# A decay table spread over 128 partitions: eight DMAs out of SBUF rows instead of one out of DRAM

## The chip, the core and the metric

The program runs on one core of a Trainium2 chip. The metric is the device time of one execution in microseconds (us). Engines are named as in the profile: PE is TensorE, DVE is VectorE, ACT is ScalarE, POOL is GpSimd, SP is SyncE; the last issues DMAs here and computes nothing.

## The reference, cut to what matters

Three parts run one after another. First comes retention attention with a decay `lam[h]` for each of 8 heads; then a mixture of 8 experts over 1536 tokens; then a two-layer network. Only the first touches the change:

```
Dmask = where(rel >= 0, lam[h] ** rel, 0)        # rel = i - j, inside a block
intra = (q_b @ k_b^T) * Dmask ; intra @ v_b
inter = (q_b * lam[h] ** (i + 1)) @ kv_state
kv_state = lam[h] ** block * kv_state + (k_b * lam[h] ** (block - 1 - j))^T @ v_b
```

The kernel uses blocks of 128 positions, which gives the same output.

## The kernel before, in words

Attention works on 12 chunks, each a block of 128 positions of all 8 heads for one of the two batches. A chunk's input is one tile `qkv` of 128 partitions by 4 x 512 floats (q and k laid out with head dimension on the partitions, then k and v with positions on the partitions; 1 MB). Four such tiles exist, so the load of chunk c + 4 is issued once `outputs(c)` has freed a tile. `load_chunk` (L169) issues a chunk in two pieces of 512 KB; chunk 0 comes as two pieces of 256 KB (q and the first k) and, later, one of 512 KB (the second k and v). All DMAs of the kernel are issued by SP, in program order, on one queue.

The decays are tabulated at the start. `g` is a tile of 8 partitions, one per head, by 384 floats: 128 zeros, then 1, then the powers lam, lam^2, ... made by one scan on DVE (L190). From it come two tables over many partitions:

- `dtab` (L196), 128 partitions x 8 heads x 128 floats, 512 KB: partition j of head h holds the 128 floats of `g`'s row h that begin at column 1 + j. So each partition reads the same row, shifted by one float.
- `lq` (L203), 128 partitions x 4 x 128 floats, 256 KB: each head's powers, the same on 64 partitions.

Neither can be read by a single DMA across `g`'s partitions in this form, so `g` is stored to a DRAM tile `gscr` (L194), and `dtab` and `lq` are read back from there.

`dtab` is used by each chunk in two places: `decay` (L242, DVE) multiplies the scores in PSUM by it, and `prep` (L227, POOL) multiplies the second k by its last column. In a chunk PE runs `scores` (L236), `states` (L258, which needs `prep`'s k), and `outputs` (L272, L277, which needs `decay`'s product). While PE has no chunk it runs matmuls on zeros, 12 at the start (L182) and 10 after the first scores (L358).

The order of the work is written out by hand; each engine runs its instructions in program order, and the framework adds the semaphore waits. From chunk 1 on, the preparation of the expert layers (splitting tokens and weights into high and low parts, L132, L133; sums of weight blocks, L109 to L112) is put between the chunks. The expert layers start on PE at L579 once the last chunks are done.

The lines of the start, in the order in which SP issues them:

```
nc.sync.dma_start(out=lamt, ...)          # L166
load_chunk(0, ((0, 1), (1, 2)))           # L176
nc.sync.dma_start(out=gscr, in_=g)        # L194
load_chunk(0, ((2, 4),))                  # L195
nc.sync.dma_start(out=dtab, in_=...gscr)  # L198
load_chunk(1)                             # L202
nc.sync.dma_start(out=lq[...], ...gscr)   # L206, twice
load_chunk(2); load_chunk(3)              # L210
nc.sync.dma_start(out=wgt, ...)           # L212
```

Of the kernel before, what the change touches and what calls it, by code (L numbers as in the profile page):

```python
# [8 lines left out]
F32 = mybir.dt.float32  # L9
# [8 lines left out]
B, H, S, D = 2, 8, 768, 64  # L18
# [32 lines left out]
def kernel(  # L51
# [9 lines left out]
    nc = tc.nc  # L61
# [20 lines left out]
    gscr = dram.tile([H, 384], F32, name="gscr")  # L82
# [78 lines left out]
    ap = attq.enter_context(tc.tile_pool(name="att", bufs=1, side="right"))  # L161
# [7 lines left out]
    def load_chunk(c, parts=((0, 2), (2, 4))):  # L169
        if c not in qkvt:  # L170
            qkvt[c] = yq.tile([128, 4, 512], F32, tag="qkv", name=f"qkv{c}")
        src = qkv[c].rearrange("p (a n) -> p a n", a=4)
        for i, j in parts:
            nc.sync.dma_start(out=qkvt[c][:, i:j], in_=src[:, i:j])
# [6 lines left out]
    for i in range(12):  # L181
        nc.tensor.matmul(out=warm, lhsT=zero[:, 0:128], rhs=zero, start=True, stop=True)  # L182
    g = hp.tile([128, 512], F32, tag="hhi", name="g")[0:H, 0:384]
# [7 lines left out]
        out=g[:, 129:257], data0=lamt.to_broadcast([H, 128]), data1=one8, initial=1.0,  # L191
        op0=ALU.mult, op1=ALU.add,
    )
    nc.sync.dma_start(out=gscr, in_=g)  # L194
    load_chunk(0, ((2, 4),))  # L195
    dtab = ap.tile([128, H, 128], F32, name="dtab")  # L196
    gbase = gscr[:, 1:129]
    nc.sync.dma_start(  # L198
        out=dtab,
        in_=bass.AP(tensor=gbase.tensor, offset=gbase.offset, ap=[[1, 128], [384, H], [1, 128]]),  # L200
    )
    load_chunk(1)  # L202
    lq = ap.tile([128, NP, 128], F32, name="lq")  # L203
    for hh in range(2):
        src = gscr[:, 129:257].rearrange("(n two) m -> two n m", two=2)[hh]
        nc.sync.dma_start(  # L206
            out=lq[64 * hh:64 * hh + 64],
            in_=src.rearrange("(o n) m -> o n m", o=1).to_broadcast([64, NP, 128]),
# [537 lines left out]
```

## Time and profile before

| what | value |
|---|---|
| median of 3 runs | 1327.33 us (1326.79 to 1328.92) |
| the profiled execution's own time | 1328.56 us |
| its span, first to last instruction | 1326.8 us |
| PE busy | 1314.7 us (99% of the span) |
| DVE busy | 913.0 us (69%) |
| ACT, POOL busy | 527.6 us (40%), 274.6 us (21%) |
| DMA traffic | 85.00 MB, mean 64 GB/s |

The engines' shares are means over the whole span. The attention part with its loads takes about the first 60 us; after it PE is busy almost without a gap until the end. The span leaves out 1.8 us of the profiled execution's time that lie before the first and after the last instruction.

### The profile page before, as it was taken

The page shows a single profiled execution, that of the slowest core. Times are in us where ns is not written, and L with a number is a line of the kernel's source. Part 1 is how long each engine was busy: PE and PEld are TensorE (multiplying, and loading weights), DVE is VectorE, ACT ScalarE, POOL GpSimd, SP SyncE. Part 2 cuts the span into 40 slices and gives each one's busy share as a digit, 9 for nine tenths or more (in the row PEclk, how much of TensorE's full clock was granted, in tenths as well). Part 3 has the DMA queues.
Part 4 walks back from the last instruction along what each step waited for, and adds up shares of the span by engine and source line. Part 5 has one row for each costly group of instructions (what it writes and reads, how often), then busy time and mean ns, then how long its engine had stood idle before and what let it go on. Part 6 is the DMA issues. An engine that isn't in the chain of part 4 may idle for free.

```text
span 1326.8 us, 20925 instructions
## 1 busy us (share of the span) xinstructions
PE 1314.7 (99%) x8383; PEld 1163.6 (88%) x8383; DVE 913.0 (69%) x1698; ACT 527.6 (40%) x1029; POOL 274.6 (21%) x323
## 2 busy tenths in 40 slices
PE   8999999999999999999999999999999999999998
PEld 6789999999999999999999999999999888888887
DVE  4976666757667575767666675757654487788887
ACT  1443333223323232323322332323232578776764
POOL 4611011212123131212212221322210102020200
PEclk8999999999999999999999999999999999999999
DMA  9501111212312121212222132221210110010101
GB/s 299 171 33 33 33 61 34 71 56 68 97 46 93 57 68 57 80 56 68 72 64 68 57 99 69 68 68 57 68 36 33 32 33 32 32 32 32 32 33 64
DMA packets 37138, 85.00 MB, mean 64 GB/s; under 512 B 4136, under 2 KB 13872, under 8 KB 37040
## 3 DMA queue, kind: packets, MB, share of 16 engines
q1 hardware_dynamic: 37040, 83.67, 19.8%
q8 instruction: 65, 1.06, 0.3%
q14 instruction: 33, 0.27, 0.1%
HBM read 72.11 MB, written 11.55 MB: 63 GB/s over the span
## 4 chain that ended last, share of the span: by engine, by line
PE 96%; DVE 2%; DMA 1%; issue 0%; ACT 0%; POOL 0%; DVEq 0%; POOLq 0%
PE yp L480 16%; PE yp L477 16%; PE yp L478 16%; PE ha L579 7%; PE ha L582 7%; PE ha L581 7%; PE hb L581 5%; PE hb L579 5%; PE hb L582 5%; PE g L688 3%; PE g L686 3%; PE g L687 3%; PE sc L236 1%; DMA dtab<-gscr 0%; DVE at L242 0%
## 5 line engine op out<-in xcount | busy, mean ns | idle before, releaser
L508 ACT ACTIVATE hhia<-ha 128x512 fp32r<-128x512 f32 x96 | 57.5, 599 | 469.9 <-PE ha L582 464.3
L579 PE MATMUL ha<-xsh,w1h 128*128 128x256 f32 x576 | 162.5, 282 | 1.8 <-ACT s L600 1.3
L582 PE MATMUL ha<-xsh,w1l 128*128 128x256 f32 x576 | 161.3, 280 | 0.0
L581 PE MATMUL ha<-xsl,w1h 128*128 128x256 f32 x576 | 160.9, 279 | 0.0
L456 POOL TENSOR_TENSOR c<-c,d 128x256 f32<-128x256 f32 x64 | 47.8, 747 | 544.3 <-DVE d L455 544.3
L478 PE MATMUL yp<-w2l,hhia 128*128 128x512 f32 x384 | 149.4, 389 | 0.0
L480 PE MATMUL yp<-w2h,hloa 128*128 128x512 f32 x384 | 149.3, 389 | 0.0
L477 PE MATMUL yp<-w2h,hhia 128*128 128x512 f32 x384 | 149.3, 389 | 0.0
L480 PE MATMUL yp<-w2h,hlob 128*128 128x512 f32 x380 | 148.6, 391 | 0.0
L478 PE MATMUL yp<-w2l,hhib 128*128 128x512 f32 x380 | 147.9, 389 | 0.0
L477 PE MATMUL yp<-w2h,hhib 128*128 128x512 f32 x380 | 147.8, 389 | 0.0
L615 DVE TENSOR_TENSOR ha<-ha,s 128x256 f32<-128x256 f32 x96 | 41.4, 432 | 141.8 <-PE ha L582 141.8
L625 DVE TENSOR_TENSOR hb<-hb,s 128x512 f32<-128x512 f32 x96 | 67.0, 698 | 91.3 <-PE hb L582 91.3
L495 DVE SCALAR_TENSOR_TENSOR yacc<-yp,prob,yacc 128x512 f32<-128x512 f32 x168 | 118.8, 747 | 9.0 <-PE yp L480 9.0
L579 PEld LDWEIGHTS ha<-xsh,w1h 128*128 128x128 f32 x576 | 108.4, 188 | 9.6 <-ACT s L600 1.5
L581 PEld LDWEIGHTS ha<-xsl,w1h 128*128 128x128 f32 x576 | 108.5, 188 | 7.4
L582 PEld LDWEIGHTS ha<-xsh,w1l 128*128 128x128 f32 x576 | 109.1, 189 | 0.0
L579 PE MATMUL hb<-xph,w1h 128*128 128x256 f32 x384 | 106.6, 278 | 0.0
L581 PE MATMUL hb<-xpl,w1h 128*128 128x256 f32 x384 | 106.3, 277 | 0.0
L582 PE MATMUL hb<-xph,w1l 128*128 128x256 f32 x384 | 106.1, 276 | 0.0
L480 PEld LDWEIGHTS yp<-w2h,hloa 128*128 128x128 f32 x384 | 72.1, 188 | 15.0
L480 PEld LDWEIGHTS yp<-w2h,hlob 128*128 128x128 f32 x380 | 71.3, 188 | 14.9
(159 smaller groups left out, 3332.6 us busy)
## 6 DMA issues: line engine op xcount, KB each, us to landing
wraw<-in_w SPq DMA_DIRECT2D x64, 512.0 KB, 4.8
d<-in_wio SPq DMA_DIRECT2D x64, 256.0 KB, 2.9
qkv<-in_qkv SPq DMA_DIRECT2D x23, 512.0 KB, 6.9
wscr<-c SPq DMA_DIRECT2D x64, 128.0 KB, 1.8
wraw<-wscr SPq DMA_DIRECT2D x16, 512.0 KB, 4.3
out<-yacc SPq DMA_DIRECT2D x12, 256.0 KB, 2.1
qkv<-in_qkv SPq DMA_DIRECT2D x2, 256.0 KB, 3.3
dtab<-gscr SPq DMA_DIRECT2D x1, 512.0 KB, 6.5
```

Of the source, the lines that this page charges most:

```text
L456: nc.gpsimd.tensor_tensor(out=c1.bitcast(F32), in0=c1.bitcast(F32), in1=lo.bitcast(F32), op=ALU.mult)
L477: nc.tensor.matmul(out=yp, lhsT=a[:, ts], rhs=w2h[q][:, i], start=first, stop=False)
L478: nc.tensor.matmul(out=yp, lhsT=a[:, ts], rhs=w2l[q][:, i], start=False, stop=False)
L480: nc.tensor.matmul(out=yp, lhsT=c[:, ts], rhs=w2h[q][:, i], start=False, stop=last)
L495: nc.vector.scalar_tensor_tensor(out=y, in0=yp[t], scalar=prob[:, b * TPB + t, u // 2:u // 2 + 1], in1=y, op0=ALU.mult, op1=ALU.add)
L508: nc.scalar.activation(out=a, in_=ps, func=ACTF.Relu)
L579: nc.tensor.matmul(out=ps, lhsT=w1h[q][:, ws], rhs=xh[:, k], start=start and k == 0, stop=False, skip_group_check=True)
L581: nc.tensor.matmul(out=ps, lhsT=w1h[q][:, ws], rhs=xl[:, k], start=False, stop=False, skip_group_check=True)
L582: nc.tensor.matmul(out=ps, lhsT=w1l[q][:, ws], rhs=xh[:, k], start=False, stop=k == 1, skip_group_check=True)
L615: nc.vector.tensor_tensor(out=pa[:, hi], in0=pa[:, lo], in1=s5, op=ALU.add)
L625: nc.vector.tensor_tensor(out=pb, in0=pb, in1=s12, op=ALU.add)
L686: nc.tensor.matmul(out=ph, lhsT=w1h[q][:, ws], rhs=x2[b][0][:, k], start=k == 0, stop=False)
```

## The change

`dtab` is no longer read from `gscr`. Eight DMAs, one for each head, read `g`'s row h in SBUF (one partition) and write all 128 partitions of `dtab[:, h]`, 128 pieces of 512 bytes, 64 KB. The even heads are issued by SP, the odd ones by ACT. They are issued right after the scan that makes `g`, ahead of the store to `gscr` and of the second half of chunk 0; `gscr` stays, since `lq` is read from it as before.

```diff
+    dtab = ap.tile([128, H, 128], F32, name="dtab")
+    for h in range(H):
+        w = g[h:h + 1, 1:129]
+        (nc.sync, nc.scalar)[h % 2].dma_start(
+            out=dtab[:, h], in_=bass.AP(tensor=w.tensor, offset=w.offset, ap=[w.ap[0], [1, 128], [1, 128]]),
+        )
     nc.sync.dma_start(out=gscr, in_=g)
     load_chunk(0, ((2, 4),))
-    dtab = ap.tile([128, H, 128], F32, name="dtab")
-    gbase = gscr[:, 1:129]
-    nc.sync.dma_start(
-        out=dtab,
-        in_=bass.AP(tensor=gbase.tensor, offset=gbase.offset, ap=[[1, 128], [384, H], [1, 128]]),
-    )
     load_chunk(1)
```

## Rows read from the trace of the kernel before

**Rows 1.** The page's part 4: the chain that ended last, shares by engine.

```profile
PE 96%; DVE 2%; DMA 1%; issue 0%; ACT 0%; POOL 0%; DVEq 0%; POOLq 0%
```

**Rows 2.** Stretches: window and length, busy us (instructions), PE clock, DMA share, GB/s.

```profile
2.00:10.00 8.00, 6.80 (x37) 3.07 (x35) 0.55 (x2) 0.22 (x2) 0.00 (x0) 1.00 0.81 223
10.00:30.00 20.00, 17.06 (x261) 14.89 (x263) 10.13 (x18) 3.73 (x7) 13.91 (x14) 0.83 1.02 346
30.00:56.00 26.00, 24.94 (x434) 20.82 (x430) 25.78 (x39) 11.14 (x23) 19.07 (x16) 1.00 0.67 234
70.00:1320.00 1250.00, 1250.00 (x7510) 1112.50 (x7510) 862.78 (x1613) 504.49 (x983) 236.32 (x282) 1.00 0.17 55
```

**Rows 3.** The chain in order of time: start us, length us, what.

```profile
0.74 1.31 DMA lamt<-in_lam
...
2.59 2.62 DMA gscr<-g
...
5.22 6.46 DMA dtab<-gscr
...
11.83 1.07 POOL qkv L227
...
12.94 1.12 PE stp L258 x16
14.07 1.71 PE o L277 x16
15.77 2.01 PE sc L236 x16
17.78 0.69 PE stp L258 x16
18.47 1.09 PE sc L236 x16
19.56 1.02 PE o L277 x16
```

**Rows 4.** Timeline of the start: start, length, engine, line, tiles [idle before, releaser].

```profile
2.15 0.41 DVE L190 TENSOR_TENSOR_SCAN g<-lamt,one 8x128 f32<-8x128 f32 x1 [0.47 <-DMA lamt<-in_lam]
2.92 0.34 SPq L174 DMA_DIRECT2D qkv<-in_qkv  x1
5.65 1.18 SPq L174 DMA_DIRECT2D qkv<-in_qkv  x2
6.47 2.33 PE L358 MATMUL still<-zero 128*128 128x512 bf16 x10
15.37 1.06 POOL L227 TENSOR_TENSOR qkv<-qkv,dtab 128x512 f32<-128x512 f32 x1 [2.48 <-DMA qkv<-in_qkv]
15.82 0.60 ACT L291 ACTIVATE xr<-o 128x512 f32<-128x512 f32 x1 [13.59 <-PE o L277]
17.78 1.28 POOL L225 TENSOR_TENSOR qd<-qkv,lq 128x512 f32<-128x512 f32 x1 [0.35 <-DMA qkv<-in_qkv]
```

**Rows 5.** Stretches of 2 us; columns as in rows 2.

```profile
10.00:12.00 2.00, 0.00 (x0) 0.00 (x0) 0.22 (x1) 0.00 (x0) 0.17 (x1) 0.77 1.00 376
...
16.00:18.00 2.00, 2.00 (x22) 1.78 (x22) 0.18 (x1) 0.42 (x1) 1.26 (x3) 0.52 1.01 397
18.00:20.00 2.00, 2.00 (x42) 1.81 (x40) 1.51 (x3) 0.00 (x0) 1.99 (x2) 1.00 1.04 392
```

**Rows 6.** DMA between 8 and 9 us: packets by size, and the queue's share.

```profile
DMA packets 307, 0.16 MB, mean 157 GB/s; under 512 B 0, under 2 KB 307, under 8 KB 307
...
q1 hardware_dynamic: 307, 0.16, 75.9%
```

**Rows 7.** SP's waits in the first 40 us: us, times, longest.

```profile
SPq L212 <- DMA qkv<-in_qkv: 1.5, 1, 1.5
SPq L174 <- DMA dtab<-gscr: 1.2, 1, 1.2
```

**Rows 8.** POOL's waits in the first 60 us: us, times, longest.

```profile
POOL qd L225 <- DMA qkv<-in_qkv: 2.9, 3, 2.3
```

## The prediction

> **What bounds the kernel now.** I read the shares of the chain first, then stretches of the span, then the chain and the timeline of the start. The chain is PE's for 96% of the span [rows 1], and from 70 to 1320 us PE has no idle time at all [rows 2]. So nothing after the attention part can absorb or add much: whatever the change does to the moment at which the expert layers start is what it does to the total.
>
> The first 60 us have three regimes. Up to 12 us the chain is DMA: `lamt` lands, DVE makes `g`, `g` takes 2.62 us to DRAM, and `dtab` takes 6.46 us from its issue at 5.22 to its landing at 11.68; at 11.83 POOL starts the first `prep` [rows 3]. From 10 to 30 us the DMA engines are full (share 1.02, 346 GB/s) beside a PE that carries the chain [rows 2, 3]. From 30 to 56 us DVE is busy for 25.78 of 26 us and the DMA share falls to 0.67 [rows 2]. A shift of the first `prep` passes through all three: PE and DVE follow it with almost no slack, and the DMA engines have slack only before 10 us, where their share is 0.81 over 8 us, a gap of 0.19 x 8 = 1.5 us [rows 2].
>
> **What is removed.** The round trip: `dtab` no longer waits for the 2.62 us of `gscr`, and its own 6.46 us go [rows 3]. The store to `gscr` itself stays, and `lq` still waits for it.
>
> **What is added on the queues.** Eight issues, four each on SP and ACT. Neighbouring issues on SP cost 0.34 us, or 0.59 each in the pair that takes 1.18 [rows 4], so four cost 1.4 to 2.4 us. On ACT they are hidden: its first work on a chunk is at 15.82 after 13.59 us of idleness [rows 4]; without that cover they would delay the first `xr` copy by these 2 us. On SP they stand in front of `gscr` and of chunk 0's second half, issued at 2.92 before [rows 4], and nothing covers that: `prep` needs that half too. There is also a wait in turn: SP's second piece of chunk 3 waited 1.2 us for `dtab`, and `wgt` 1.5 us for a piece of `qkv` [rows 7]. In the list of issues each of these stands exactly eight behind what it waits for. If that count runs over both queues together, heads 6 and 7 wait for chunk 0's first pieces, and then `gscr`, chunk 0's second half and both pieces of chunk 1 wait for heads 0 to 3 to land, the `lq` reads for heads 4 and 5, chunk 2 for heads 6 and 7. So all loads hang on how fast the eight land.
>
> **What the eight reads cost.** No transfer of before goes from SBUF to SBUF, so I bound it. Each head moves 128 x 512 B = 65,536 B, all eight 524,288 B.
>
> Lower end: the rate of full loads, 392 GB/s [rows 5], gives 1.34 us. Next to it stands the rate of the same 512 B pieces as they come from DRAM: 307 in 1 us at 157 GB/s [rows 6], which gives 3.3 us.
>
> Upper end: the source is 8 of 128 partitions. In the full loads 128 partitions together take 392 GB/s [rows 5], so eight take a sixteenth, 24.5 GB/s, which is also one DMA engine's rate. No row shows eight partitions moving more. At that rate a head takes 2.67 us and all eight 21.4 us. Farther still, a single partition's share is 3.06 GB/s: if one head at a time went at that, the eight would take 171 us. And if small pieces held a shared source to what one engine does with them, 157 / 16 / 0.76 = 12.9 GB/s [rows 6], it would be 40.6 us.
>
> The destination and the pieces are as before; what is new is the source, 128 readers of one partition. So I go by the row on how many bytes a few partitions move, 24.5 GB/s for the eight, and take 21.4 us.
>
> The Trainium skill speaks against this change at the same place. Its page "SBUF — State Buffer", section "Door 1: The DMA port swizzle (why [64,N] ≈ [32,N])", says that a DMA's bandwidth follows from how many of SBUF's 16 ports its partitions reach, that partitions 0 to 3 lie behind one port and 4 to 7 behind another, and that four partitions were measured at 27.6 GB/s. By it heads 0 to 3 would take 262,144 B / 27.6 GB/s = 9.5 us and heads 4 to 7 as long again, 9.5 us if both halves ran at once and 19.0 us in the order of issue, an estimate. No run so far shows a read of so few partitions.
>
> **The sum.** `g` is ready at 2.56 us [rows 4]; the smallest DMA takes 1.31 us from issue to landing [rows 3], so data flow by 2.59 + 1.31 = 3.9 us. The eight are done at 3.9 + 21.4 = 25.3 us. Chunk 0's second half is behind them on the same queue: 524,288 B at 392 GB/s, 1.3 us, 26.6 us. `prep` followed the landing by 0.15 us [rows 3]: 26.8 us instead of 11.83, 15.0 us late. What is late next: chunk 1 is there at 26.6 + 2.7 = 29.3 us against 15.37 [rows 4], 13.9 late, which that shift covers; the `lq` reads (256 KB, about 0.8 us) and chunk 2 (2.7 us) end at about 32.8 us against 17.78 [rows 4], 15.0 late. All three agree, so the whole part moves by 15 us. PE idles longer, from the end of the zero matmuls at 8.80 [rows 4] to about 28 us, but its clock had already fallen in the short pause of before (granted 0.77 between 10 and 12, 0.52 between 16 and 18, 1.00 from 18 on [rows 5], that is to 1.2 GHz and back to 2.4), so the same slow stretch is paid again, not a new one.
>
> 1328.56 + 15.0 = 1343.6 us for an execution like the profiled one; that one lay 1.2 us above the median, so against the median I say **1342 us**, 1.1% slower.
>
> **Rivals.**
>
> *The rows are read at the rate of other transfers, and it is faster.* The place is `dtab`'s landing; the point that decides is 11.68 us, that is 524,288 B in 7.8 us, 67 GB/s, if chunk 0's second half comes in time too. For it: the 512 B pieces from DRAM, 1,536 B of one row shared by 128 readers there too, came at 157 GB/s [rows 6]. Against it: eight partitions. Then `dtab` lands at 3.9 + 1.3 to 3.3 = 5.2 to 7.2 us, chunk 0's second half, put back by the issues and the wait in turn, at perhaps 9, and `prep` starts 2.8 us earlier. PE's pause shrinks, and its slow stretch (1.12 + 1.71 + 2.01 us against 0.69 + 1.02 + 1.09 at full clock [rows 3]) can give back 2.0 more. But the loads from 10 to 30 us can come earlier only by what fills the gap before, 1.5 us, and POOL already waited up to 2.3 us for `qkv` [rows 8]. So 1.5 to 4.8 us, say 2.5: 1325 us.
>
> The Trainium skill has a rule on this side too: "DMA: Bandwidth & Descriptors", section "Why small descriptors are slow (HBM only)", says that SBUF to SBUF transfers do not suffer from small descriptors. By it the eight would come nearer to the 1.34 us of the full rate; the 512 B packets of rows 6 do run slow, and they come from DRAM, so the trace agrees as far as it goes.
>
> *Two rows are read at a time,* one from each queue, each at 24.5 GB/s: 10.7 us, `dtab` at 14.6, chunk 0's second half at 15.9, `prep` 4.2 us late: 1331.5 us. For it: the two queues are independent. Against it: the rows of the same moment are neighbours.
>
> *Nothing changes that can be measured:* a read of about 7 us ends where the old one did, or an earlier `dtab` is eaten by the later second half of chunk 0: 1326 to 1329 us.
>
> **The numbers.** Chances: 0.50 for the forecast or slower still, 0.13 for two rows at a time, 0.27 for the faster rival, 0.10 for no change. About 0.2%, 2.7 us, is what a measurement can tell from no change. The faster rival lies on that bound and is split, 0.16 beyond and 0.11 within; of the case without change 0.03 is slower. So faster 0.16, same 0.18, slower 0.66. The likeliest case's own range runs from 24.5 + a fifth, 29.4 GB/s (17.8 us, 3.6 less: 1338) to halfway between 24.5 and 12.9, 18.7 GB/s (28.0 us, 6.6 more: 1349). For 8 in 10 the range must take in the two-at-a-time case, no change and most of the faster one: 1324 to 1349. Some 0.1 lies below; 0.1 lies above, with the ends of 40.6 us and 171 us.
>
> **What would show it.** Right: `dtab`'s eight DMAs take several us each from issue to landing, in steps of some 2.7 us; POOL's first `prep` waits until past 20 us; the DMA rate between 4 and 25 us is a small part of 223 GB/s; afterwards chain and loads look as before, shifted. Wrong: `dtab` lands before 11 us and the wait in front of `prep` becomes one for `qkv`; or the rate of the eight is far from 24.5 GB/s; or part of the shift is taken back between 30 and 60 us, if DVE's stretch has more slack than 0.2 us.

## The result, and the profile after

The changed kernel takes 1341.54 us (median of 4 runs, 1340.27 to 1342.32) against 1327.37 us (4 runs, 1326.79 to 1328.92): a ratio of 1.0105, 95% interval 1.0092 to 1.0118, or 14.2 us. The profiled execution of after took 1341.58 us at a span of 1339.8 us, 13.0 us more than that of before.

The page's part 4 of the changed kernel. SP's issues have become a part of the chain, where before they were none [rows 1]:

```profile
PE 95%; DVE 2%; DMA 1%; SPq 1%; issue 0%; ACT 0%; DVEq 0%
```

Stretches of the changed kernel (columns as in rows 2). The first three cover the reads of the table; the last three answer to [rows 2], each 14 us later:

```profile
6.00:13.00 7.00, 2.91 (x22) 1.35 (x19) 0.00 (x0) 0.00 (x0) 0.00 (x0) 1.00 0.65 27
13.00:15.00 2.00, 0.00 (x0) 0.00 (x0) 0.00 (x0) 0.00 (x0) 0.00 (x0) 0.83 0.62 55
15.00:21.00 6.00, 0.00 (x0) 0.00 (x0) 0.00 (x0) 0.00 (x0) 0.00 (x0) 0.50 0.59 25
...
24.00:44.00 20.00, 16.57 (x250) 14.39 (x252) 9.00 (x17) 3.73 (x7) 13.41 (x13) 0.82 1.00 346
44.00:70.00 26.00, 24.69 (x440) 20.80 (x437) 25.90 (x39) 10.67 (x22) 18.93 (x17) 1.00 0.66 231
84.00:1334.00 1250.00, 1250.00 (x7505) 1112.70 (x7504) 862.07 (x1614) 503.90 (x981) 236.50 (x282) 1.00 0.17 55
```

The reader sees three things. From 6 to 21 us the DMA engines move 25 to 27 GB/s, and about twice that between 13 and 15, where the reads pass from the rows of heads 0 to 3 to those of heads 4 to 7. The share of busy time (0.59 to 0.65) does not show it: before, a share of 0.76 went with 157 GB/s [rows 6]. And the later stretches are nearly those of before, in rates and in busy times.

The timeline of the changed kernel's start (columns as in rows 4):

```profile
2.60 11.64 SPq L198 DMA_DIRECT2D dtab<-g  x4
2.61 8.73 ACTq L198 DMA_DIRECT2D dtab<-g  x4
...
14.29 4.34 SPq L201 DMA_DIRECT2D gscr<-g  x1
18.67 3.23 SPq L174 DMA_DIRECT2D qkv<-in_qkv  x3
...
23.32 1.29 DVE L243 TENSOR_TENSOR at<-sc,dtab 128x512 f32<-128x512 f32 x2 [20.60 <-DMA qkv<-in_qkv]
...
25.54 1.06 POOL L228 TENSOR_TENSOR qkv<-qkv,dtab 128x512 f32<-128x512 f32 x1 [24.09 <-DMA qkv<-in_qkv]
...
26.65 1.12 PE L259 MATMUL stp<-qkv 128*64 128x64 f32 x16 [17.74 <-POOL qkv L228]
...
30.03 1.06 POOL L228 TENSOR_TENSOR qkv<-qkv,dtab 128x512 f32<-128x512 f32 x1 [3.43 <-DMA qkv<-in_qkv]
...
32.43 1.27 POOL L226 TENSOR_TENSOR qd<-qkv,lq 128x512 f32<-128x512 f32 x1 [0.38 <-DMA qkv<-in_qkv]
```

The first `prep` starts at 25.54 us instead of 11.83 [rows 3], 13.7 us late; `prep` of chunk 1 at 30.03 instead of 15.37 and `qd` of chunk 2 at 32.43 instead of 17.78 [rows 4], 14.7 us late. Four issues hold SP for 11.6 us; the store to `gscr` and then chunk 0's second half come only after them. That half, not the table, is what the first `prep` waits for in the end: it lands 6.5 us after its issue, at 25.2 us. The last piece of the table to land is head 6, which SP issues at 10.46 us (issues between 10.6 and 11.2 us, with KB each and us to landing):

```profile
dtab<-g SPq DMA_DIRECT2D x1, 64.0 KB, 12.7
```

So the table is whole at 23.2 us. DVE's first product with it starts at 23.32; the profile puts that wait down to a load of `qkv`, but the scores that the product also needs had been ready since 6.6 us.

In the two profiled executions, a part of the shift is given back at the beginning of the expert layers. The chain of the changed kernel, and the same place in that of before (start, length, what):

```profile
78.70 0.39 PE ha L580
...
81.10 0.99 PE lgT L329 x32
```

```profile
64.16 0.39 PE ha L579
...
67.17 1.83 PE lgT L328 x32
```

At the first pair the shift is 14.54 us, at the second 13.93, and behind the second, whose work takes 0.84 us less, it is the 13.0 us of the span. The pause in front of the first pair is the same, 1.3 us of idle time in both (timelines of before and of after):

```profile
64.16 0.39 PE L579 MATMUL ha<-xsh,w1h 128*128 128x256 f32 x1 [1.32 <-ACT s L600]
```

```profile
78.70 0.39 PE L580 MATMUL ha<-xsh,w1h 128*128 128x256 f32 x1 [1.32 <-ACT s L601]
```

After it PE's clock fell to half (0.50, that is 1.2 GHz) in before and not in after (stretches of before, of after, and of the first experiment below, in which the eight read DRAM; columns as in rows 2):

```profile
66.00:68.00 2.00, 2.00 (x26) 1.55 (x29) 0.72 (x2) 1.31 (x3) 0.00 (x0) 0.50 0.00 0
```

```profile
80.00:82.00 2.00, 1.86 (x38) 1.54 (x38) 0.79 (x2) 1.86 (x4) 0.00 (x0) 1.00 0.04 8
```

```profile
66.00:68.00 2.00, 2.00 (x41) 1.65 (x40) 1.59 (x4) 1.66 (x5) 0.00 (x0) 1.00 0.04 8
```

Nothing shows that the change took that half clock away: the experiment's attention part is as early as that of before, and its clock does not fall there either. Of all the kernels profiled here, only before and the one with its rows in every fourth partition show it at this place. The profiled execution of before lay 1.2 us above its median, and by the medians the shift is 14.2 us, close to the 14.54 at the first pair.

### The profile page after: what moved, and what is told of

Same layout as the page of the kernel before. It is cut to its first block, busy times and chain, and to the rows that moved or that the text cites. A ratio compares the mean times of both kernels' runs of the same rounds, so it can differ in the third digit from the quotient of the medians.

```text
span 1339.8 us, 20940 instructions
## 1 busy us (share of the span) xinstructions
PE 1313.1 (98%) x8383; PEld 1163.2 (87%) x8383; DVE 912.5 (68%) x1698; ACT 527.9 (39%) x1029; POOL 274.7 (21%) x323
## 4 chain that ended last, share of the span: by engine, by line
PE 95%; DVE 2%; DMA 1%; SPq 1%; issue 0%; ACT 0%; DVEq 0%
PE yp L481 16%; PE yp L478 16%; PE yp L479 16%; PE ha L580 7%; PE ha L583 7%; PE ha L582 7%; PE hb L582 5%; PE hb L580 5%; PE hb L583 5%; PE g L689 3%; PE g L687 3%; PE g L688 3%; SPq L198 1%; DMA qkv<-in_qkv 1%; DMA gscr<-g 1%
```

## The experiments

Three theories stood against each other. Theory 1: the source is the limit, since few neighbour partitions together give some 25 GB/s. Theory 2: 128 readers of one row, each shifted by 4 bytes, are slow wherever the row lies. Theory 3: eight small DMAs from two queues are slow whatever they read, or SBUF is a slow source as such. Ratios are to the kernel before on the same chip.

| run | us | ratio, 95% interval |
|---|---|---|
| the eight read DRAM | 1326.88 | 0.9996 (0.9986 to 1.0005) |
| rows in partitions 0, 4, ... 28 | 1330.66 | 1.0028 (1.0018 to 1.0038) |
| no shift | 1341.76 | 1.0107 (1.0087 to 1.0127) |
| source of 128 partitions | 1326.69 | 0.9999 (0.9990 to 1.0009) |
| all eight from ACT | 1338.62 | 1.0081 (1.0064 to 1.0098) |
| rows in partitions 0 to 3 and 32 to 35 | 1345.72 | 1.0134 (1.0113 to 1.0156) |
| table by scan | 1324.06 | 0.9976 (0.9967 to 0.9985) |
| both tables by scan | 1322.53 | 0.9969 (0.9957 to 0.9980) |

**The eight read DRAM.**

```diff
-        w = g[h:h + 1, 1:129]
+        w = gscr[h:h + 1, 1:129]      # moved behind the store to gscr and chunk 0's second half
```

> The eight DMAs, their size and the two queues stay, but they read the heads' rows in gscr, in DRAM, after the store to it. Theory 1 (few partitions: the eight rows lie in 8 neighbour partitions, which together give about 25 GB/s): the source is gone, so the table lands within 2 us of before's 11.7 us and the time is that of before, 1325 to 1330 us. Theory 2 (128 readers of one row, each shifted by 4 bytes, are slow wherever the row lies): still slow, 1338 us or more. Theory 3 (eight small DMAs from two queues, put in turn, are slow whatever they read): 1336 us or more.

1326.88 us, the time of before. The first `prep` of this kernel, in its timeline:

```profile
11.56 1.06 POOL L228 TENSOR_TENSOR qkv<-qkv,dtab 128x512 f32<-128x512 f32 x1 [10.11 <-DMA dtab<-gscr]
```

Eight DMAs, 64 KB each, two queues, 128 shifted readers of one row: all of it is there, and nothing is slow. Theories 2 and 3 fall, as far as theirs is a cost of any source. This run also puts the eight behind chunk 0's second half; the next one keeps them where the change has them.

**A source of 128 partitions.**

```diff
-            out=dtab[:, h], in_=bass.AP(tensor=w.tensor, offset=w.offset, ap=[w.ap[0], [1, 128], [1, 128]]),
+            out=dtab[:, h], in_=ones,
```

> The eight DMAs, two queues and place stay, but each copies a tile of 128 partitions of ones in SBUF, 512 bytes from each; the table is all ones, the decays are left out of it. Theory 1: nothing is slow about SBUF as a source, so the eight move at 157 to 392 GB/s, the table lands at 5.5 to 8 us, and the time is 1322 to 1327 us. Theory 3, or SBUF to SBUF being slow as such: 1336 us or more.

1326.69 us: SBUF is no slow source as such. The timeline of this kernel, and a wait from its list of SP's waits:

```profile
2.09 3.27 SPq L198 DMA_DIRECT2D dtab<-ones  x4
6.66 0.31 SPq L199 DMA_DIRECT2D gscr<-g  x1
7.01 1.30 SPq L174 DMA_DIRECT2D qkv<-in_qkv  x3
...
12.07 1.06 POOL L225 TENSOR_TENSOR qkv<-qkv,dtab 128x512 f32<-128x512 f32 x1 [10.62 <-DMA qkv<-in_qkv]
```

```profile
SPq L199 <- DMA dtab<-ones: 1.2, 1, 1.2
```

It also says why the change would have brought nothing even with a fast read. The table is no longer waited for, but the wait in front of the first `prep` has gone over to chunk 0's second half: behind four issues and a wait in turn it is issued at 7.01 us instead of 2.92 [rows 4], and `prep` starts at 12.07 us.

**No shift.**

```diff
-        w = g[h:h + 1, 1:129]
+        w = g[h:h + 1, 128:256]
...
-            ap=[w.ap[0], [1, 128], [1, 128]]
+            ap=[w.ap[0], [0, 128], [1, 128]]
```

> All 128 partitions read the same 512 bytes of a head's row, which begin at a multiple of 512 bytes in the tile; the shift by one float for each partition is left out. Theory 1: the bytes and the partitions are the same, so the eight move at 25 GB/s (at most 30 if shifted pieces cost more): 1338 to 1342 us. Theory 2: the shift was the cost, and the time falls to 1325 to 1330 us.

1341.76 us, as with the shift. DMA from 6 to 12 us, first the changed kernel, then this one:

```profile
DMA packets 334, 0.15 MB, mean 25 GB/s; under 512 B 37, under 2 KB 334, under 8 KB 334
```

```profile
DMA packets 347, 0.16 MB, mean 26 GB/s; under 512 B 40, under 2 KB 347, under 8 KB 347
```

Shifted pieces cost at most 1 GB/s in 26. Theory 2 is out also for a source in SBUF.

**Rows in every fourth partition.**

```diff
-        w = g[h:h + 1, 1:129]
+        w = g[4 * h:4 * h + 1, 1:129]      # g: 32 partitions; lam goes to every fourth
```

> Everything as in the changed kernel, but the eight rows lie in partitions 0, 4, 8, ... 28 instead of 0 to 7. Theory 1, in the form that four neighbour partitions share 25 GB/s: the two rows that are read at the same time (one for each queue) lie in different groups, so the eight move at about 50 GB/s, 10.5 us instead of some 17; the first prep starts at 15 to 19 us and the time is 1330 to 1335 us. If a row in one partition were the limit by itself, or theory 2 or 3 held, nothing would change: 1340 to 1343 us.

1330.66 us, at the lower end of what theory 1 gave. DMA of this kernel from 6 to 9 us, and its first `prep`:

```profile
DMA packets 645, 0.29 MB, mean 98 GB/s; under 512 B 70, under 2 KB 645, under 8 KB 645
```

```profile
14.88 1.06 POOL L229 TENSOR_TENSOR qkv<-qkv,dtab 128x512 f32<-128x512 f32 x1 [13.40 <-DMA qkv<-in_qkv]
```

The same eight rows, four partitions apart, are read at 98 GB/s instead of 25, which takes back 10.9 of the 14.2 us. I had reckoned with two rows at a time and 50 GB/s; it was twice that, which would be about four rows at once. What stays of the loss is again chunk 0's second half.

**Rows 32 partitions apart.**

```diff
-        w = g[h:h + 1, 1:129]
+        p = 32 * (h % 2) + h // 2          # even heads in 0 to 3, odd heads in 32 to 35
+        w = g[p:p + 1, 1:129]             # g: 64 partitions; lam and gscr move in two DMAs each
```

> The even heads' rows lie in partitions 0 to 3, the odd ones' in 32 to 35, so the two rows that are read at the same time are always 32 partitions apart. Theory 1 with groups of neighbour partitions: two groups are read at once, 50 GB/s, 1330 to 1335 us. Theory 1 with the groups of the Trainium skill's page SBUF - State Buffer, section Door 1: The DMA port swizzle, by which 0 to 3 and 32 to 35 lie behind one port: all eight rows share 25 GB/s from the first to the last, without the stretch of 50 to 59 GB/s that the changed kernel has between 13 and 15 us: 1341 to 1345 us.

1345.72 us (two runs), 0.7 above the 1341 to 1345 expected and not faster than the changed kernel. The intervals of the two ratios touch, but the trace agrees that it is slower: the first `prep` starts at 29.83 us against 25.54. Part of that need not be the reads: the eight are issued 0.5 us later, and the store to `gscr` is two DMAs. Its stretch from 6 to 25 us:

```profile
6.00:25.00 19.00, 3.23 (x26) 1.67 (x24) 0.00 (x0) 0.00 (x0) 0.00 (x0) 0.65 0.65 24
```

24 GB/s throughout, without the stretch of double rate that the changed kernel has. Partitions 0 to 3 and 32 to 35 share one path, while 0 to 3 and 4 to 7 do not. The Trainium skill's page "SBUF — State Buffer", section "Door 1: The DMA port swizzle (why [64,N] ≈ [32,N])", puts 0 to 3 and 32 to 35 behind one port and gives a port about 27 GB/s; these runs agree, with 24 to 27 GB/s, on reads.

**All eight from ACT.**

```diff
-        (nc.sync, nc.scalar)[h % 2].dma_start(
+        nc.scalar.dma_start(
```

> All eight DMAs are issued by ACT, none by SP, so the loads and the store to gscr no longer stand behind them on SP's queue. What the read rate alone costs and what the queue behind it costs come apart. Theory 1: the eight still move at about 25 GB/s, one row at a time, and the table lands at 22 to 25 us, but chunks 0 to 3 and lq have landed by then, so the first prep follows the table at once and no load is waited for in the chunks after it: 1336 to 1341 us, some 1 to 5 us under the changed kernel. If SP's queue were most of the loss, it would fall to 1333 us or less.

1338.62 us, 2.9 us under the changed kernel. Its ACT queue, SP's loads and the first `prep`s:

```profile
2.62 14.67 ACTq L198 DMA_DIRECT2D dtab<-g  x8
```

```profile
2.96 7.83 SPq L174 DMA_DIRECT2D qkv<-in_qkv  x3
14.32 4.56 SPq L207 DMA_DIRECT2D lq<-gscr  x2
```

```profile
24.49 2.07 POOL L228 TENSOR_TENSOR qkv<-qkv,dtab 128x512 f32<-128x512 f32 x2 [23.04 <-DMA lq<-gscr]
```

Against what I expected, the loads are not free of the slow reads on the other queue. SP's issues themselves are short: the three of 7.83 us take 0.34, 0.33 and 0.40 us, and the rest is waiting (SP's waits in the first 30 us: us, times, longest):

```profile
SPq L174 <- DMA qkv<-in_qkv: 6.7, 2, 4.5
SPq L207 <- DMA dtab<-g: 4.4, 2, 3.5
```

`lq` does not read `dtab`. The first of the two waits at L207 can also be one for `gscr`, which `lq` does read; the second, at 15.95 us, cannot, since the first read of `gscr` had been issued by then. So SP waits in turn for a DMA that ACT issued. Chunks 0 and 1 are nevertheless both there when the table is, and two `prep`s run back to back. The profile puts the wait of the first one down to `lq`, which it does not use; DVE's first product with the table starts at 23.52 us, and why `prep` follows only 1 us later is open. So of the 14.2 us some 11 are the reads, with what they still cost the loads, and some 3 come from standing in front of the loads on SP's queue.

**The table made in place.** If the start waits for table and loads, a table that is not moved must help. One DMA spreads `lam` over 128 partitions (`lamb`), and DVE, idle then, makes each head's table by a scan that a 1 on the anti-diagonal (`imp`) starts.

```diff
-    for h in range(H): ...dma_start(out=dtab[:, h], in_=...)
     nc.sync.dma_start(out=gscr, in_=g)
     load_chunk(0, ((2, 4),))
+    for h in range(H):
+        nc.vector.tensor_tensor_scan(
+            out=dtab[:, h], data0=lamb[:, h:h + 1].to_broadcast([128, 128]), data1=imp, initial=0.0,
+            op0=ALU.mult, op1=ALU.add)
     load_chunk(1)
```

> The decay table is not moved at all: lam is spread to 128 partitions by one small DMA, and eight scans on DVE make the table in place, each head's powers started by a 1 on the anti-diagonal; chunk 0's second half is issued right after the store to gscr, lq is read from gscr as before. If the start is bound by the table and the loads, as the runs so far say, the first prep starts at 7 to 8 us instead of 11.8, the DMA engines move 0.5 MB less while they are full, and the time is 1321 to 1325 us. If DVE's stretch from 30 us on alone sets the end of the attention part, or the loads from 10 to 30 us do and cannot come earlier, the time stays at 1326 to 1328 us.

1324.06 us, faster than both kernels. The scans and the first `prep` in its timeline:

```profile
3.79 2.63 DVE L205 TENSOR_TENSOR_SCAN dtab<-lamb,imp 128x128 f32<-128x128 f32 x8 [1.18 <-DMA lamb<-in_lam]
```

```profile
7.50 1.06 POOL L234 TENSOR_TENSOR qkv<-qkv,dtab 128x512 f32<-128x512 f32 x1 [5.54 <-DMA qkv<-in_qkv]
```

**Both tables made in place.** `lq` by four more scans; `g`, `gscr` and the DMAs that touch them are gone.

```diff
-    nc.sync.dma_start(out=gscr, in_=g)
...
-        nc.sync.dma_start(out=lq[...], in_=...gscr...)
+    for n in range(NP):
+        nc.vector.tensor_tensor_scan(
+            out=lq[:, n], data0=lamq[:, n:n + 1].to_broadcast([128, 128]), data1=one8, initial=1.0,
+            op0=ALU.mult, op1=ALU.add)
```

> As the run before, and lq is made by four more scans on DVE; g, gscr and all three DMAs that touch it are gone. If the loads between 10 and 30 us are what holds the chunks, another 0.25 MB less and no wait of SP for gscr give 0.5 to 1.5 us more than the run before: 1320 to 1324 us. If not, it is the same as the run before within 0.5 us.

1322.53 us, 4.4 us under before on the same chip (1326.92). The 1.5 us between these two runs are as expected. Their intervals overlap, but five of the six runs lie below all eleven of the run before, on the same chip, so that step is likely. The first `prep` starts at 7.60 us, 4.2 earlier than before, and the product that the chain of before has at 64.16 us starts at 58.01 (these two executions lie 6.3 us apart, more than the medians). The stretches of this kernel show what is left:

```profile
2.00:10.00 8.00, 7.15 (x48) 3.44 (x47) 5.50 (x17) 0.22 (x2) 1.06 (x1) 1.00 0.92 313
10.00:30.00 20.00, 19.15 (x350) 16.46 (x348) 14.04 (x26) 4.86 (x10) 15.15 (x15) 1.00 1.00 369
```

The gap in the DMA engines before 10 us is mostly filled (0.92 against 0.81 [rows 2]), PE's clock never falls before 30 us, and the loads are full from 10 us on as before.

## Why the prediction was right, step by step

- **What bounds the kernel:** right. From 84 to 1334 us PE has no idle time, and the stretches of the attention part came back almost unchanged, 14 us later.
- **The cost of the reads:** the mechanism was right, and the rate too: 24.5 GB/s foreseen for eight of 128 partitions, 25 to 27 measured while one group of four is read. The size of the term was off: the slow stretch ended at some 21 us and the last piece landed at 23.2, not at 25.3, since the rows lie in two groups whose reads overlap for 2 us. Where all eight share one path (the run with rows 32 apart), they move at 24 GB/s, close to the rate of the sum. The sign that I had named, landings in steps of 2.7 us, did not come: several heads were under way at once, and each took 9.7 to 15.3 us from issue to landing.
- **The queue behind:** the order was right, the size too small. Chunk 0's second half was to land 1.3 us after the table; it landed 2.0 us after it, at 25.2, because four issues and the store to `gscr` held SP until 18.67 us. I had put the four issues at 1.4 to 2.4 us; they lasted 11.6. The two errors, 2.1 us too long for the table and 0.7 too short behind it, partly cancel: `prep` at 25.54 us against 26.8 foreseen. That the total lands within 1 us of 1342 is to this extent luck.
- **The wait in turn over both queues:** the run with a fast source shows it, SP's store waiting 1.2 us for a piece of the table. The run with all eight on ACT shows it from one queue to the other. In the changed kernel itself no wait for a piece of the table is listed: SP was held until 14.29 us, and head 0 had landed at 12.3.
- **The shift passes through:** right up to the expert layers, 14.5 us, and in the medians, 14.2. The 1.5 us by which the two profiled executions come closer after that belong to a half clock in the one of before, a stretch that I had not looked at. That PE's longer pause at the start would cost no more than the short one was right: the slow stretch after it is there once, as before.
- **The faster rival:** its point was right (the rate of the source decides; out of 128 partitions the table's pieces moved at 270 GB/s between 5 and 6 us), its price was not. With a fast source the second half of chunk 0 comes at 11.7 us, not at the 9 that I gave it, and nothing is gained. The step of this rival that failed is the cost of putting four issues in front of that load.
- **The rival of two rows at a time:** it holds for 2 us, between 13 and 15. Its reason, that the two queues are independent, is not borne out: with all eight on ACT the loads on SP's queue came later too.

## What to carry to other kernels

Price a DMA that spreads a few SBUF rows over all partitions by the partitions that it reads, and not by its bytes alone: here eight neighbours gave some 25 GB/s, the same rows four partitions apart 98, and the detour over DRAM 157. The busy share of the DMA engines did not show the limit, the GB/s did. And a DMA put in front of a load that the first work needs moved the wait to that load; the table that an idle engine made in place cost neither.

## What the runs showed of the hardware that was not expected

- A DMA's issue can hold the issuing engine for several us when what it issued before drains slowly: SP's four issues took 11.6 us and ACT's four 8.7, a single one up to 6.05, against 0.47 to 0.65 us for each of the same eight with a source of 128 partitions. The list of waits does not show it. That the queue was full is inferred, not shown.
- Slow reads on one queue came with slower loads on the other: with all eight on ACT, chunk 0's second half took 7.4 us from issue to landing, against 5.0 before, though it was issued at the same time (2.96 and 2.92 us).
- A pause of PE of the same 1.3 us was followed by a half clock (0.50, 1.2 GHz) in one execution and by the full one (2.4 GHz) in another; what decides is not shown here.
